# An RWKV-7 recurrence with a SoLU expert layer on one core: only TensorE in a written order, fences as drains, 32-blocks read back from DRAM, decays computed transposed

## The chip, the cores and the metric

The kernel runs on one core of a Trainium2 chip. The metric is device time in microseconds (us) of one execution. The kernel before takes 964.93 us, the median of 3 runs (963.79 to 968.83). All arithmetic is in 32-bit floats. TensorE has two clock levels, 1.2 and 2.4 GHz; the profile's "clock" is the granted share of the higher one.

## The reference

The first half is a recurrence over 768 time steps for 4 batches and 8 heads of dimension 40, on a 40x40 state per head. The second half takes its output, 3072 tokens of 320 numbers, through a layer with an activation, a layer norm and a second matrix.

```python
for t in range(S):                       # S = 768, state [4, 8, 40, 40]
    y[:, :, t] = einsum('bhd,bhde->bhe', r[t], state)
    Sa = einsum('bhde,bhe->bhd', state, a[t])
    state = state * w[t] - einsum('bhd,bhe->bhde', Sa, b[t])
    state = state + einsum('bhd,bhe->bhde', v[t], k[t])

h = x @ w_in                             # [3072, 320] @ [320, 1024]
e = exp(h - max(h))
solu = h * e / (sum(e) + 1e-9)
ln = (solu - mean) / sqrt(var + 1e-6) * g_ln
out = ln @ w_out                         # [3072, 1024] @ [1024, 320]
```

The expert weights come as 64-bit floats; the kernel reads their bits and rebuilds 32-bit floats itself.

## The kernel before

**Chunks.** The 768 steps are cut into 12 chunks of 64, and the 4 batches into 2 pairs, which makes 24 chunk-steps that run one after the other, the two pairs in turn. A pair's two batches lie in the two halves of the 128 partitions. Within a chunk the recurrence becomes small matrix products per batch and head (32 matmuls of one kind at a time, all through the helper `mm`, L212) and a triangular 64x64 solve per batch and head. The solve uses the inverses of the two 32x32 diagonal blocks.

**Names.** `pnt`/`nt` is the triangular matrix of a chunk (`norm`), evicted from PSUM by VectorE. `decay` takes the logarithm of w (`lw`), sums it over time with a matmul (`pcum`) and makes `inv`, its negative exponential, and `ei`, its exponential; four matmuls in `front` turn `ei` into `pex`, which ScalarE copies to `ex`. `kb` (GpSimd) goes to DRAM and comes back rearranged as `kbx`. `px` is the right side of the solve, `x0` its copy (ScalarE), `pu` the solved values, `py` and `pz` the products that build the lower left block of the inverse in `tinvT`. `pyo` holds the chunk's output and the new state; `leave` turns it into `x` and, through four DMAs, `xT`; `tot` and `st` are the new state. `h`, `nmax`, `e`, `bs`, `mv`, `c`, `rs` (GpSimd), `lnT`, `po` and `osb` belong to the expert layer, which runs one and two chunk-steps behind the recurrence.

**Inversion.** The 32x32 blocks of four chunk-steps (4 x 32 of them) make one tile `blk` with a block in each partition. `invert` turns it on VectorE into the inverse `u` with 30 pairs of instructions (`prod`, L358, then `u`, L360), copies its transpose on GpSimd (L363) and writes both to DRAM; `bring` reads the pieces for a step. There are six inversions. Their pieces are laid between the other work by calls `some(k)`. The blocks reach `blk` by six DMAs a step into `blk_dram` (`spread`, L337 and L342) and one load a group (L347).

**Order.** `manual_schedule()` (L83) makes every engine execute its instructions in the order in which the program writes them. The main loop counts i from -9 to 25. Step i begins the matrix work of chunk-step j = i+7 (`norm`), loads its successors, and finishes chunk-step i. For i < 0 only early work is done, and the weights are converted there, five pieces a step (`drawn(5)`). SyncE issues all the DMAs but the weights'.

**Fences.** Before matmuls of another row group add into a PSUM bank, `fence` (L215) puts an empty instruction on GpSimd's queue that takes the bank's tile; TensorE's next matmul then waits for GpSimd to come to it. It stands in `carried` (tiles of `px`) and in the first `read` (tiles of `pyo`), two fences a step. GpSimd works in the program's order too.

Of the kernel before, what the change touches and what calls it, by code (L numbers as in the profile page):

```python
# [45 lines left out]
def kernel(  # L46
# [36 lines left out]
    ctx.enter_context(tc.manual_schedule())  # L83
# [25 lines left out]
    ei_t = zeroed(nc.vector, "ei", [P, H, C], 2, pad)  # L109
    kb_t = zeroed(nc.gpsimd, "kb", [P, 2 * H, C], 2, pad)  # L110
    ex_t = zeroed(nc.vector, "ex", [P, 2, 4, C + 1], AHEAD + 2, lambda x: x[:, :, :, 0:1])
# [21 lines left out]
    def narrow(dst, bits):  # L133
# [4 lines left out]
        def tmp(name):  # L138
            return two.tile([P, 320], I32, tag="n_" + name, name="n_" + name)[0:n, 0:width]

        man, scale, low = tmp("man"), tmp("scale"), tmp("low")
# [89 lines left out]
    def src(ap, i, p):  # L231
        bp, ci = where_(i)
        return ap[2 * bp + p, :, ci * C:(ci + 1) * C, :].rearrange("h t d -> t h d")
# [5 lines left out]
    def load_keys(i, queue=None):  # L239
        if not ok(i):  # L240
            return
        d = st[i]
        for n, ap in (("w", w), ("b", b), ("k", k), ("a", a)):
            x = a_t[i % 3] if n == "a" else two.tile([P, H, D], FP32, tag="raw_" + n, name="raw_" + n)
            d["raw_" + n] = x
            for p in range(2):
                (queue or nc.sync).dma_start(out=x[half(p), :, 0:D], in_=src(ap, i, p))  # L247

    def load_values(i):
        if not ok(i):  # L250
            return
        d = st[i]
        d["v"], d["r"] = v_t[i % 2], r_t[i % 2]
        for n, ap in (("v", v), ("r", r)):
            for p in range(2):
                for h in range(2):
                    nc.sync.dma_start(out=d[n][half(p), 4 * h:4 * h + 4, 0:D], in_=src(ap, i, p)[:, h::2])  # L257


    def decay(i):  # L260
# [3 lines left out]
        lw = two.tile([P, H, D], FP32, tag="lw", name="lw")  # L264
        nc.scalar.activation(out=lw, in_=d["raw_w"], func=AF.Ln)  # L265
        t = bank("pcum")
        nc.tensor.matmul(t[:, 0:DM], lhsT=c_("cum"), rhs=lw, start=True, stop=True)  # L267
        inv = two.tile([P, DM], FP32, tag="inv", name="inv")
        nc.scalar.activation(out=inv, in_=t[:, 0:DM], func=AF.Exp, scale=-1.0)
        d["ei"] = ei_t[i % 2]  # L270
        nc.scalar.activation(out=d["ei"][:, :, 0:D], in_=heads(t[:, 0:DM]), func=AF.Exp)
# [15 lines left out]
    def front(i):  # L287
        if not ok(i):
# [25 lines left out]
    def norm(i):  # L314
# [11 lines left out]
        n, at = i // GRP, (i % GRP) * 32  # L326
        if i % GRP == 0:
            blocks[n] = dram.tile([P, Q, Q], FP32, tag="blk_dram", name="blk_dram", bufs=2)

    def spread(i):  # L330
        if not ok(i):
            return
        nt, n, at = st[i]["nt"], i // GRP, (i % GRP) * 32
        for x in range(2):
            lo = slice(C * x, C * x + Q)
            hi = slice(C * x + Q, C * x + C)
            nc.sync.dma_start(out=blocks[n][at + 8 * x:at + 8 * x + 8].rearrange("h s t -> s h t"),  # L337
                              in_=nt[lo, :, :, 0:Q].rearrange("s h j t -> s (h j) t"))
            base = at + 16 + 4 * x
            gap = 12 if x == 0 else 4  # L340
            for h in range(2):
                nc.sync.dma_start(out=blocks[n][base + gap * h:base + gap * h + 4].rearrange("h s t -> s h t"),  # L342
                                  in_=nt[hi, h, :, Q:])

    def invert(n):
        nb = two.tile([P, Q, Q], FP32, tag="blk", name="blk", bufs=1)
        nc.sync.dma_start(out=nb, in_=blocks[n])  # L347
        u = two.tile([P, Q, Q], FP32, tag="u", name="u", bufs=1)
        flat = u.rearrange("p s t -> p (s t)")
        nc.vector.tensor_scalar(out=flat, in0=nb.rearrange("p s t -> p (s t)"), scalar1=-1.0, scalar2=None,  # L350
                                op0=ALU.mult)
        nc.vector.memset(flat[:, 0:Q * Q:Q + 1], 1.0)
# [9 lines left out]
        ut = nb  # L362
        nc.gpsimd.tensor_copy(out=ut, in_=u.rearrange("p s t -> p t s"))  # L363
        inverse[n] = []
        for name, x in (("u_dram", u), ("ut_dram", ut)):
            x_dram = dram.tile([P, Q, Q], FP32, tag=name, name=name, bufs=2)
            nc.sync.dma_start(out=x_dram, in_=x)
            inverse[n].append(x_dram)
# [3 lines left out]
    def bring(i):  # L372
# [3 lines left out]
        d["ti"], d["ul"], d["uh"] = ti_t[i % 2], ul_t[i % 2], uh_t[i % 2]  # L376
        u, ut = inverse[i // GRP]
        at = (i % GRP) * 32
        for x in range(2):
            lo = slice(C * x, C * x + Q)  # L380
            hi = slice(C * x + Q, C * x + C)
            nc.sync.dma_start(out=d["ul"][lo].rearrange("s h j t -> s (h j) t"),
                              in_=ut[at + 8 * x:at + 8 * x + 8].rearrange("h s t -> s h t"))
            base = at + 16 + 4 * x
            for h in range(2):
                nc.sync.dma_start(out=d["uh"][hi, h], in_=u[base + 8 * h:base + 8 * h + 4].rearrange("h s t -> s h t"))
            nc.sync.dma_start(out=d["ti"][lo, :, :, 0:Q].rearrange("s h j t -> s (h j) t"),
                              in_=u[at + 8 * x:at + 8 * x + 8].rearrange("h s t -> s h t"))
# [8 lines left out]
    def couple(i):  # L397
# [12 lines left out]
    def close(i):  # L410
# [4 lines left out]
        for u in in_turn(lambda p, g, q, h: (p, p ^ h)):  # L415
            p, g, q, h = u
            j = 2 * g + q
            mm(t[h][half(p ^ h), j * Q:j * Q + Q], wy[half(p), h, j], d["uh"][half(p), h, j])
        for h in range(2):
            nc.scalar.copy(out=d["ti"][:, h, :, Q:], in_=t[h][:, 0:4 * Q].rearrange("p (j c) -> p j c", j=4))  # L420


    def attend(i):
# [6 lines left out]
        d["lv"] = two.tile([P, H, W2], FP32, tag="lv", name="lv")  # L430
        nc.gpsimd.tensor_copy(out=d["lv"][:, :, C:], in_=d["v"][:, :, 0:D])
# [21 lines left out]
    def carried(i):  # L453
# [7 lines left out]
        if ci:  # L461
# [6 lines left out]
            fence(d["px"])  # L468
# [14 lines left out]
    def solved(i):  # L483
# [47 lines left out]
    def read(i, own):  # L531
# [212 lines left out]
```

## Time and profile before

| | us |
|---|---|
| median of 3 runs | 964.93 |
| the profiled execution | 965.61 |
| its span | 963.8 |
| TensorE busy | 645.0 |
| VectorE busy | 388.8 |
| ScalarE busy | 248.1 |
| GpSimd busy | 146.9 |
| mean granted clock | 0.787 |

The span goes from the first to the last instruction of the profiled execution. No engine is busy for much more than two thirds of it. The kernel has three stretches: up to the first `h` at 230.7 us, where the early chunk-steps and the weights are prepared; the 24 `h` from 230.7 to 942.8 us, one per chunk-step; and the last 21.0 us. Five of the six inversions lie beside the second stretch. A step is best measured from one start of `h` to the next. TensorE waits seldom long, but the granted clock falls after it has been idle, and then the same matmuls take longer.

### The profile page before, as it was taken

What the parts mean: (1) busy time and instruction counts of PE and PEld (TensorE: products, weight loads), DVE (VectorE), ACT (ScalarE), POOL (GpSimd) and SP (SyncE); (2) the same over time, 40 slices, a digit from 0 to 9 for tenths busy, and PEclk for the clock granted to TensorE, in tenths of its full rate; (3) what the DMA queues carried; (4) which work ended last, traced back from release to release, by engine and by line L of the source; (5) the groups of instructions that cost most, each with busy time, mean ns of one, the idle gap of its engine ahead of it and who ended that gap; (6) DMA issues with size and microseconds to landing.
All of it is one profiled execution on the core that took longest, in us unless ns stands there. A gap on an engine that the chain in (4) does not pass through costs nothing.

```text
span 963.8 us, 27077 instructions
## 1 busy us (share of the span) xinstructions
PE 645.0 (67%) x11449; PEld 479.1 (50%) x11449; DVE 388.8 (40%) x1046; ACT 248.1 (26%) x616; POOL 146.9 (15%) x191
## 2 busy tenths in 40 slices
PE   1422124447797657988287876679893888888886
PEld 1311113435565355666265654556673666666653
DVE  2433464125633095412456330954127442333221
ACT  1322012212333132323123331323220322222211
POOL 4535233000121011011001210110200001000000
PEclk7565555656799869999598998598985877777879
DMA  6545343534344324354143543242431123222000
GB/s 132 141 101 122 90 106 100 108 66 100 85 135 112 77 65 102 63 147 107 40 106 90 138 111 78 65 101 36 130 84 58 27 59 98 56 54 53 20 14 18
DMA packets 245016, 81.86 MB, mean 85 GB/s; under 512 B 227736, under 2 KB 234784, under 8 KB 244896
## 3 DMA queue, kind: packets, MB, share of 16 engines
q1 hardware_dynamic: 242784, 74.64, 33.3%
q10 hardware_dynamic: 2112, 5.49, 1.8%
q8 instruction: 91, 1.49, 0.6%
q14 instruction: 29, 0.24, 0.1%
HBM read 50.19 MB, written 25.95 MB: 79 GB/s over the span
## 4 chain that ended last, share of the span: by engine, by line
PE 26%; issue 22%; DVE 20%; SPq 11%; DMA 9%; POOL 7%; ACT 4%; ACTq 0%; POOLq 0%; DVEq 0%
PE h L599 7%; PE po L649 6%; DVE prod L358 4%; SPq L257 3%; DVE u L360 3%; POOL n_scale L144 2%; PE pyo L212 2%; PE plnT L639 2%; DVE nmax L602 2%; DMA blk<-blk_dram 2%; SPq L247 2%; DMA bits<-in_moe_w_in_dram 2%; DVE e L611 2%; ACT e L605 2%; DVE bs L619 2%
## 5 line engine op out<-in xcount | busy, mean ns | idle before, releaser
L602 DVE TENSOR_REDUCE nmax<-h 128x1 f32<-128x1024 f32 x24 | 29.4, 1223 | 278.1 <-PE h L599 278.1
L599 PE MATMUL h<-w_in,xT 120*128 120x512 f32 (+1 forms) x288 | 136.0, 623 | 0.0
L649 PE MATMUL po<-w,lnT 128*128 128x320 f32 x384 | 114.5, 453 | 0.2 <-ACT lnT L640 0.2
L628 POOL TENSOR_TENSOR rs<-c,mhalf 128x1 f32<-128x1 f32 x24 | 13.7, 571 | 597.0 <-DVE c L627 575.4
L267 PE MATMUL pcum<-lw,cst 128*128 128x320 f32 x48 | 26.6, 647 | 97.4 <-ACT lw L265 97.4
L649 PEld LDWEIGHTS po<-w,lnT 128*128 128x128 f32 x384 | 76.2, 205 | 30.4 <-issue 4.5
L599 PEld LDWEIGHTS h<-w_in,xT 120*128 120x128 f32 (+1 forms) x288 | 55.1, 198 | 62.5 <-issue 59.8
L605 ACT ACTIVATE e<-h,nmax 128x1024 f32<-128x1024 f32 x24 | 26.8, 1116 | 195.6 <-DVE nmax L602 195.6
L212 PE MATMUL pyo<-lv,kbx 64*64 64x104 f32 x768 | 43.6, 295 | 43.5 <-POOLq L217 31.2
L358 DVE TENSOR_TENSOR prod<-blk,u 128x30 f32<-128x30 f32 (+9 forms) x180 | 68.5, 381 | 5.3
L360 DVE TENSOR_TENSOR u<-u,prod 128x30 f32<-128x30 f32 (+9 forms) x180 | 66.0, 367 | 6.2
L350 DVE TENSOR_SCALAR u<-blk 128x1024 f32<-128x1024 f32 x6 | 4.2, 694 | 146.5 <-DMA blk<-blk_dram 146.5
L267 PEld LDWEIGHTS pcum<-lw,cst 128*128 128x128 f32 x48 | 9.6, 250 | 104.5 <-ACT lw L265 104.5
L212 PEld LDWEIGHTS pyo<-lv,kbx 64*64 64x64 f32 x768 | 27.6, 159 | 47.3 <-POOLq L217 33.5
L481 ACT COPY x<-px 128x160 f32<-128x160 f32 x48 | 11.7, 295 | 140.6 <-PE px L212 140.6
L280 PE MATMUL paT<-cst,a 128*104 128x128 f32 x96 | 19.0, 335 | 42.8 <-DVE lu L304 42.8
L212 PE MATMUL px<-lv,psi 64*64 64x40 f32 x768 | 22.2, 275 | 36.9 <-POOLq L217 36.7
L212 PE MATMUL pyo<-lu,kbx 64*64 64x104 f32 x768 | 42.4, 289 | 0.7 <-DVE lu L304 0.5
L639 PE MATMUL plnT<-cst,e 128*128 128x128 f32 x192 | 40.2, 376 | 3.9 <-DVE e L611 3.9
L212 PE MATMUL pnt<-aT,bT 40*64 40x64 f32 x768 | 20.9, 259 | 28.2 <-DVE aT L299 27.7
L212 PEld LDWEIGHTS px<-lv,psi 64*64 64x64 f32 x768 | 19.7, 185 | 39.4 <-issue 34.1
L280 PE MATMUL pkT<-cst,kbx 128*104 128x128 f32 x96 | 22.7, 382 | 23.0 <-DMA kbx<-kb_dram 22.9
(105 smaller groups left out, 1196.3 us busy)
## 6 DMA issues: line engine op xcount, KB each, us to landing
kb_dram<-kb SPq DMA_DIRECT2D x24, 512.0 KB
kbx<-kb_dram SPq DMA_DIRECT2D x24, 512.0 KB
raw_w<-in_w_dram SPq DMA_DIRECT2D x50, 80.0 KB
raw_b<-in_b_dram SPq DMA_DIRECT2D x50, 80.0 KB
raw_k<-in_k_dram SPq DMA_DIRECT2D x50, 80.0 KB
a<-in_a_dram SPq DMA_DIRECT2D x50, 80.0 KB
v<-in_v_dram SPq DMA_DIRECT2D x96, 40.0 KB
r<-in_r_dram SPq DMA_DIRECT2D x96, 40.0 KB
```

Source lines behind the costliest of these rows:

```text
L144: nc.gpsimd.tensor_scalar(out=scale, in0=scale, scalar1=1023 - 127, scalar2=1023 + 128, op0=ALU.max, op1=ALU.min)
L212: nc.tensor.matmul(o, lhsT=lhsT, rhs=rhs, start=start, stop=stop, skip_group_check=True)
L257: nc.sync.dma_start(out=d[n][half(p), 4 * h:4 * h + 4, 0:D], in_=src(ap, i, p)[:, h::2])
L267: nc.tensor.matmul(t[:, 0:DM], lhsT=c_("cum"), rhs=lw, start=True, stop=True)
L280: nc.tensor.transpose(out=t[0:W2, j * P:(j + 1) * P], in_=pair(src_, 2 * j), identity=ident)
L358: nc.vector.tensor_tensor(out=t, in0=nb[:, j:j + 1, j + 1:Q].to_broadcast([P, j, m]), in1=u[:, 0:j, j:j + 1].to_broadcast([P, j, m]), op=A ...
L360: nc.vector.tensor_tensor(out=u[:, 0:j, j + 1:Q], in0=u[:, 0:j, j + 1:Q], in1=t, op=ALU.subtract)
L599: nc.tensor.matmul(h[:, hh], lhsT=d["xT"][0:n, kt, :], rhs=w_in[0:n, kt, hh], start=kt == 0, stop=kt == NK - 1)
L602: nc.vector.tensor_reduce(out=nmax, in_=h, axis=AX.X, op=ALU.max, negate=True)
L605: nc.scalar.activation(out=e, in_=h, func=AF.Exp, bias=nmax, accum_out=d["esum"])
L639: nc.tensor.transpose(out=t[:, j * P:(j + 1) * P], in_=d["e"][:, f * P:(f + 1) * P], identity=ident)
L649: nc.tensor.matmul(o[:, 0:DM], lhsT=d["lnT"][:, f, :], rhs=w2[:, f, :], start=f == 0, stop=f == NF - 1)
```

## The change

Only TensorE keeps the written order. The order of the other engines is set by a scheduler at build time, which is why the rows below and not the diff show it. A fence becomes a drain instruction on TensorE itself. `nt` is written whole to DRAM (one DMA) and its blocks come back into `blk` by four DMAs a step; `blk` has two buffers. v and r are loaded by four DMAs instead of eight and put in order by GpSimd copies. `u` and its transpose lie side by side in one tile, so that `bring` needs four DMAs instead of eight. Of the four xT DMAs two are issued by ScalarE. The output is one DMA. `pex` is computed from `lw` against the summing matrix, so that `ei` and its transposes go. The weights' pieces are drawn in steps -4 to -1, nine a step, the rest in step 0. SyncE issues 26 DMAs in a plain step, before 38.

```diff
-    ctx.enter_context(tc.manual_schedule())
+    ctx.enter_context(tc.manual_schedule(engines={mybir.EngineType.PE}))
...
-    def fence(tiles):
-        for t in tiles:
-            nc.gpsimd.keepalive_nop([nc.gpsimd.lower_ap(t[:, 0:512])])
+    def fence():
+        nc.tensor.drain()
...
+    def in_value_order(i):
...
+        d["v"], d["r"] = v_t[i % 2], r_t[i % 2]
+        d["lv"] = two.tile([P, H, W2], FP32, tag="lv", name="lv")
+        for x, n in ((d["v"][:, :, 0:D], "raw_v"), (d["r"][:, :, 0:D], "raw_r"), (d["lv"][:, :, C:], "raw_v")):
+            nc.gpsimd.tensor_copy(out=x.rearrange("p (h x) d -> p h x d", h=2),
+                                  in_=d[n].rearrange("p (x h) d -> p h x d", h=2))
...
-        nc.scalar.activation(out=d["ei"][:, :, 0:D], in_=heads(t[:, 0:DM]), func=AF.Exp)
+        t = bank("pex")
+        for j in range(4):
+            nc.tensor.matmul(t[0:W2, j * P:(j + 1) * P], lhsT=pair(lw, 2 * j), rhs=c_("cum"), start=True, stop=True)
+        ex = d["ex"] = ex_t[i % (AHEAD + 3)]
+        nc.scalar.activation(out=ex[0:W2, :, :, 1:].rearrange("p b j t -> p j b t"),
+                             in_=t[0:W2].rearrange("p (j b t) -> p j b t", j=4, b=2), func=AF.Exp)
...
+        d["nt_dram"] = dram.tile([P, H, C], FP32, tag="nt_dram", name="nt_dram", bufs=3)
+        nc.sync.dma_start(out=d["nt_dram"], in_=nt.rearrange("p h j c -> p (h j) c"))
...
+        if at == 0:
+            blocks[n] = two.tile([P, Q, Q], FP32, tag="blk", name="blk")
+        for e in range(2):
+            for x in range(2):
+                lo, home = C * x + Q * e, 32 * at + 16 * e + 8 * x
+                nc.sync.dma_start(out=blocks[n][home:home + 8],
+                                  in_=st[i]["nt_dram"][lo:lo + Q, :, Q * e:Q * e + Q].rearrange("s h t -> h s t"))
...
-        nb = two.tile([P, Q, Q], FP32, tag="blk", name="blk", bufs=1)
-        nc.sync.dma_start(out=nb, in_=blocks[n])
+        nb = blocks[n]
+        uu = two.tile([P, Q, 2, Q], FP32, tag="uu", name="uu", bufs=1)
...
+            nc.sync.dma_start(out=d["tu"][lo, :, 0:2 * Q],
+                              in_=uu[at + 8 * x:at + 8 * x + 8].rearrange("h s t -> s h t"))
+            nc.sync.dma_start(out=d["uh"][hi],
+                              in_=uu[at + 16 + 8 * x:at + 24 + 8 * x, :, Q:].rearrange("h s t -> s h t"))
...
-            nc.sync.dma_start(out=xT[2 * D:3 * D, h, :], in_=x[C * h:C * h + D, 3, :])
+            nc.scalar.dma_start(out=xT[2 * D:3 * D, h, :], in_=x[C * h:C * h + D, 3, :])
...
-        if early:
-            drawn(5)
+        if -4 <= i < 0:
+            drawn(9)
...
-        if i == -1:
+        if i == 0:
             drawn(100)
```

**VectorE around an inversion.** Before, in a step that ends a group of four, the inversion begins right behind `nt` (evicted norm), and the step's row maximum of `h`, `nmax`, stands behind its sixth pair. Its beginning:

```order
L583 TENSOR_TENSOR tot<-pyo,st_130 104x4x40 x2
L304 TENSOR_TENSOR nt<-pnt,cst 128x256 x2
L350 TENSOR_SCALAR u<-blk 128x1024
L352 MEMSET u 128x32
L358 TENSOR_TENSOR prod<-blk,u 128x30
```

Eight rows of the same kind follow, and then the sixth pair and `nmax`:

```order
L358 TENSOR_TENSOR prod<-blk,u 128x150
L360 TENSOR_TENSOR u<-u,prod 128x6x25
L602 TENSOR_REDUCE nmax<-h 128x1
L304 TENSOR_TENSOR lu<-pl,cst 128x4x64 x2
L611 TENSOR_TENSOR e<-h,e 128x1024
L304 TENSOR_TENSOR psi<-ps,cst 128x256 x2
```

After, the inversion (on the joint tile `uu`) begins one step later, again right behind `nt`, and `nmax` stands behind 49 of its 62 instructions. Its beginning:

```order
L576 TENSOR_TENSOR tot<-pyo,st_131 104x4x40 x2
L312 TENSOR_TENSOR nt<-pnt,cst 128x256 x2
L353 TENSOR_SCALAR uu<-blk 128x32x32
L354 MEMSET uu 128x32
L360 TENSOR_TENSOR prod<-blk,uu 128x30
```

The place of `nmax`, 46 rows further on:

```order
L362 TENSOR_TENSOR uu<-uu,prod 128x23x8
L360 TENSOR_TENSOR prod<-blk,uu 128x168
L595 TENSOR_REDUCE nmax<-h 128x1
L312 TENSOR_TENSOR lu<-pl,cst 128x4x64 x2
L362 TENSOR_TENSOR uu<-uu,prod 128x24x7
L360 TENSOR_TENSOR prod<-blk,uu 128x150
L604 TENSOR_TENSOR e<-h,e 128x1024
```

So `nmax`, on which `e` and the expert layer of the step rest, has moved from behind the sixth pair to behind the twenty-third; with the step's delay all four quarters of `blk` were loaded a step earlier.

**SyncE between `nt` and `blk`.** Before, in the step that ends a group, the six writes of blocks and the load of the whole stand behind the loads of keys, v and r.

```order
L257 DMA v_124<-in_v_dram 64x4x40 x4
L257 DMA r_120<-in_r_dram 64x4x40 x4
L337 DMA blk_dram<-nt 32x8x32
L342 DMA blk_dram<-nt 32x4x32 x2
L337 DMA blk_dram<-nt 32x8x32
L342 DMA blk_dram<-nt 32x4x32 x2
L347 DMA blk<-blk_dram 128x1024
L395 DMA kbx<-kb_dram 128x1024
```

After, one write of `nt` goes ahead of these loads, and the four reads of blocks behind them; they are there in every step.

```order
L335 DMA nt_dram<-nt 128x512
L232 DMA raw_w<-in_w_dram 64x8x40 x2
L232 DMA raw_b<-in_b_dram 64x8x40 x2
L232 DMA raw_k<-in_k_dram 64x8x40 x2
L232 DMA a_79<-in_a_dram 64x8x40 x2
L232 DMA raw_v<-in_v_dram 64x8x40 x2
L232 DMA raw_r<-in_r_dram 64x8x40 x2
L346 DMA blk<-nt_dram 8x32x32 x4
L390 DMA kbx<-kb_dram 128x1024
```

The loads of v and r have become two of two instead of two of four, and the quarter of `blk` of a step comes in that step.

**ScalarE between `s` and `kT`.** Here `tinvT` (after: `tu`) takes the product `pz`, `x` is the right side copied from `px`, and `xT` the transfer of the step's output. Before:

```order
L529 COPY s<-psT 104x512
L420 COPY tinvT_132<-pz 128x4x32 x2
L481 COPY x_144<-px 128x4x40 x2
L640 COPY lnT<-plnT 128x512 x2
L284 COPY kT<-pkT 104x512
```

After:

```order
L522 COPY s<-psT 104x512
L415 COPY tu_135<-pz 128x4x32 x2
L568 DMA xT<-x 40x128 x2
L474 COPY x_143<-px 128x4x40 x2
L633 COPY lnT<-plnT 128x512 x2
L295 COPY kT<-pkT 104x512
```

Two issues of xT, which wait for VectorE's `x`, now stand ahead of ScalarE's copy of `px` and of `lnT`.

## Rows read from the trace of the kernel before

**Rows 1.** The page, its first line.
```profile
span 963.8 us, 27077 instructions
```

**Rows 2.** Windows cut at starts of h; columns: stretch, its length, busy time, clock, DMA share.
```profile
0.00:230.70 230.70, 80.26 (x1046) 61.27 (x1046) 94.30 (x269) 47.68 (x119) 75.88 (x92) 0.60 0.47 107
365.70:498.40 132.70, 97.98 (x1937) 72.23 (x1929) 58.59 (x154) 38.22 (x98) 15.60 (x21) 0.87 0.41 96
757.20:897.40 140.20, 116.77 (x2185) 89.35 (x2180) 45.76 (x124) 38.01 (x96) 10.40 (x16) 0.81 0.23 57
```

**Rows 3.** Windows: a plain step, a step with the head of an inversion, the tail.
```profile
265.40:291.80 26.40, 22.59 (x489) 16.57 (x483) 8.79 (x23) 10.15 (x28) 5.23 (x6) 1.00 0.46 126
450.60:498.40 47.80, 26.80 (x488) 20.10 (x483) 23.17 (x61) 9.53 (x25) 3.47 (x5) 0.75 0.34 76
942.80:963.80 21.00, 12.49 (x37) 6.74 (x35) 4.28 (x8) 3.33 (x6) 0.55 (x1) 0.90 0.07 16
```

**Rows 4.** Timeline, TensorE, plain step; columns: start, length, instructions, [idle before <-releaser].
```profile
278.20 0.41 PE L212 MATMUL pyo<-lv,kbx 64*64 64x104 f32 x8 [0.47 <-POOLq L217]
...
280.88 0.68 PE L212 MATMUL px<-lv,psi 64*64 64x40 f32 x32 [0.80 <-POOLq L217]
...
291.20 0.66 PE L212 MATMUL py<-ul,nt 64*64 64x32 f32 x30 [1.51 <-DMA ul<-ut_dram]
```

**Rows 5.** Timeline, VectorE, the same plain step.
```profile
270.86 1.23 DVE L602 TENSOR_REDUCE nmax<-h 128x1 f32<-128x1024 f32 x1 [12.95 <-PE h L599]
...
280.47 0.74 DVE L304 TENSOR_TENSOR nt<-pnt,cst 128x256 f32<-128x256 f32 x2
```

**Rows 6.** Waits of the whole span: engine, what waited, releaser, total, times, longest.
```profile
DVE u L350 <- DMA blk<-blk_dram: 146.5, 6, 31.9
...
PE px L212 <- POOLq L217: 36.7, 20, 3.6
...
PE pyo L212 <- POOLq L217: 31.2, 20, 3.3
```

**Rows 7.** Timeline, VectorE, the step with the head of an inversion.
```profile
440.65 0.74 DVE L304 TENSOR_TENSOR nt<-pnt,cst 128x256 f32<-128x256 f32 x2
468.95 0.69 DVE L350 TENSOR_SCALAR u<-blk 128x1024 f32<-128x1024 f32 x1 [27.55 <-DMA blk<-blk_dram]
...
473.05 1.22 DVE L602 TENSOR_REDUCE nmax<-h 128x1 f32<-128x1024 f32 x1
...
480.57 1.04 DVE L358 TENSOR_TENSOR prod<-blk,u 128x184 f32<-128x184 f32 x1
```

**Rows 8.** Timeline, SyncE's queue, the same step.
```profile
465.76 0.34 SPq L347 DMA_DIRECT2D blk<-blk_dram  x1
```

**Rows 9.** Timeline, TensorE, the same step.
```profile
474.65 1.10 PE L280 MATMUL paT<-cst,a 128*104 128x128 f32 x4 [16.04 <-DVE lu L304]
```

**Rows 10.** Groups of instructions, VectorE; count, busy time, mean ns of one.
```profile
L358 DVE TENSOR_TENSOR prod<-blk,u 128x30 f32<-128x30 f32 (+9 forms) x180 | 68.5, 381 | 5.3
L360 DVE TENSOR_TENSOR u<-u,prod 128x30 f32<-128x30 f32 (+9 forms) x180 | 66.0, 367 | 6.2
```

**Rows 11.** Timeline, TensorE, a step from 757 us on.
```profile
827.92 0.62 PE L212 MATMUL pyo<-lv,kbx 64*64 64x104 f32 x8 [3.30 <-POOLq L217]
```

**Rows 12.** Groups of instructions, TensorE: the matmuls behind the second fence.
```profile
L212 PE MATMUL pyo<-lv,kbx 64*64 64x104 f32 x768 | 43.6, 295 | 43.5 <-POOLq L217 31.2 <-DVE lu L304 11.4 <-ACT ei L271 0.9
```

**Rows 13.** Groups of instructions, GpSimd: the copy of v.
```profile
L431 POOL COPY lv<-v 128x320 f32<-128x320 f32 x24 | 11.1, 461 | 2.2 <-DMA v<-in_v_dram 2.2
```

**Rows 14.** Timeline, VectorE, first inversion, before the main loop.
```profile
103.67 0.69 DVE L350 TENSOR_SCALAR u<-blk 128x1024 f32<-128x1024 f32 x1 [7.93 <-DMA blk<-blk_dram]
```

**Rows 15.** Timeline, TensorE, from the first inverse to the first h.
```profile
167.74 0.39 PE L212 MATMUL py<-ul,nt 64*64 64x32 f32 x2 [1.63 <-DMA ul<-ut_dram]
...
189.13 1.07 PE L280 MATMUL pkT<-cst,kbx 128*104 128x128 f32 x4 [11.28 <-DMA kbx<-kb_dram]
...
214.73 0.44 PE L212 MATMUL pyo<-lv,kbx 64*64 64x104 f32 x2 [11.42 <-DVE lu L304]
```

More of the change, by code (lines that the diff above doesn't have):

```diff
@@ L229, in where_, with load, load_keys @@
         return i % NPAIR, i // NPAIR
-    def src(ap, i, p):
+    def load(x, ap, i):
         bp, ci = where_(i)
-        return ap[2 * bp + p, :, ci * C:(ci + 1) * C, :].rearrange("h t d -> t h d")
+        for p in range(2):
+            nc.sync.dma_start(out=x[half(p), :, 0:D],
+                              in_=ap[2 * bp + p, :, ci * C:(ci + 1) * C, :].rearrange("h t d -> t h d"))
     def ok(i):
         return 0 <= i < N
-    def load_keys(i, queue=None):
+    def load_keys(i):
         if not ok(i):
@@ L245, in load_keys @@
             d["raw_" + n] = x
-            for p in range(2):
-                (queue or nc.sync).dma_start(out=x[half(p), :, 0:D], in_=src(ap, i, p))
+            load(x, ap, i)
     def load_values(i):
@@ L252, in load_values @@
         d = st[i]
+        for n, ap in (("v", v), ("r", r)):
+            d["raw_" + n] = two.tile([P, H, D], FP32, tag="raw_" + n, name="raw_" + n)
+            load(d["raw_" + n], ap, i)
+    def in_value_order(i):
+        if not ok(i):
+            return
+        d = st[i]
         d["v"], d["r"] = v_t[i % 2], r_t[i % 2]
[L254 to L257, printed above, removed]
+        d["lv"] = two.tile([P, H, W2], FP32, tag="lv", name="lv")
+        for x, n in ((d["v"][:, :, 0:D], "raw_v"), (d["r"][:, :, 0:D], "raw_r"), (d["lv"][:, :, C:], "raw_v")):
+            nc.gpsimd.tensor_copy(out=x.rearrange("p (h x) d -> p h x d", h=2),
+                                  in_=d[n].rearrange("p (x h) d -> p h x d", h=2))
     def decay(i):
@@ L361, in invert @@
             yield
-        ut = nb
         nc.gpsimd.tensor_copy(out=ut, in_=u.rearrange("p s t -> p t s"))
[L364 to L368, printed above, removed]
+        inverse[n] = dram.tile([P, Q, 2 * Q], FP32, tag="uu_dram", name="uu_dram", bufs=2)
+        nc.sync.dma_start(out=inverse[n], in_=uu.rearrange("p s two t -> p s (two t)"))
         yield
@@ L649, in output @@
             nc.tensor.matmul(o[:, 0:DM], lhsT=d["lnT"][:, f, :], rhs=w2[:, f, :], start=f == 0, stop=f == NF - 1)
-        osb = two.tile([P, DM], FP32, tag="osb", name="osb")
+        osb = two.tile([P, DM], FP32, tag="osb", name="osb", bufs=1)
         nc.scalar.activation(out=osb, in_=o[:, 0:DM], func=AF.Copy, scale=d["rs"])
-        for p in range(2):
-            row = (2 * bp + p) * S + ci * C
-            nc.sync.dma_start(out=out[row:row + C, :], in_=osb[half(p)])
+        nc.sync.dma_start(out=out.rearrange("(b s) n -> b s n", b=B)[2 * bp:2 * bp + 2, ci * C:ci * C + C], in_=osb)
     inv, wts = [None], weights()
@@ L674 @@
             load_keys(0)
-            load_keys(1)
         carried(i)
```

86 lines of the change are left out of this document (29 added, 57 removed).

## The prediction

> **What bounds the kernel now.** I read the span first [rows 1], then windows cut at starts of `h` [rows 2], one step without and one with the head of an inversion [rows 3], and last the timelines of the engines in these. Three things are to be seen. The first `h` comes at 230.7 us, and TensorE is busy for 80 of these at a clock of 0.60. A cycle of four steps takes 132.7 us, of which a step with the head of an inversion takes 47.8 and a plain one 26.4: 3 x 26.4 + 47.8 = 127, and the rest is in the step behind the head. And from 757 us on, where no early work is left, five steps take 140.2 us, 28.0 each, longer than the plain step with all its early work, at a clock of 0.81 against 1.00.
>
> In the plain step TensorE is busy for 22.59 of 26.40 us, so it is the bound, and 3.81 us are gaps. Three of them are 0.47 and 0.80 us behind the fences and 1.51 us at `py`, which waits for a piece of the inverse that SyncE sent late [rows 4]. Over the span the fences hold TensorE for 36.7 + 31.2 us, up to 3.6 us at a time [rows 6]: GpSimd reaches the empty instruction only when it has done what stands ahead of it. In the late steps one such gap is 3.30 us [rows 11]. In the step with the inversion's head VectorE has `nt` at 441.39, then waits 27.55 us for `blk`, runs six pairs and starts `nmax` at 473.05 [rows 7], whereas TensorE stands 16.04 us at `paT`, behind `lu`, which is queued behind `nmax` [rows 9]. The load of `blk` is issued at 465.76, 24.4 us behind `nt`, because SyncE's queue holds the loads of the inputs first [rows 8].
>
> **The change, part by part.** All sums are for the profiled execution, 965.61 us, which is 1.8 over its span and 0.7 over the median.
>
> *Drains.* A plain step has two; the one in `carried` is absent in the first chunks, so there are 22 + 24 = 46. No drain is in the trace. From below the cost is 0 (GpSimd's fences could only be met at once). The nearest row for the inside of one is a `pyo` matmul, 0.295 us [rows 12], which must end before the next starts, while consecutive ones overlap; with the next weight load uncovered I take 0.45 us. The upper end is the present gap, 3.30 us. So 46 x 0.45 = 20.7 us, and 0 to 152 as bounds.
>
> The Trainium skill ("TensorE: Matmul & The Clock Gate", section "Single matmul latency") gives an isolated matmul of N columns (398 + N) / 2.4 ns at the high clock. By that an uncovered one of 104 columns would be 0.21 us and the 46 drains 9.6 us, 11 us less than by the row; no row here shows an isolated one.
>
> *A plain step with early work.* 26.40 - 1.51 (SyncE issues 26 DMAs a step instead of 38, so the pieces of the inverse leave earlier) - 0.47 - 0.80 (the two old fences) + 2 x 0.45 = 24.5 us. The new order of ScalarE puts two issues of xT ahead of `x0` and `lnT`; I cost them at nothing, since TensorE works on `pnt` and `pyo` meanwhile; without that cover they are rival B. One transpose group and one ScalarE exponential go, four `pex` matmuls take the place of four transposes: no change. Of the steps from the first `h` on, 14 are of this kind (343 us), and the two in which the early work ends take 23.0 each (46).
>
> *Late steps.* Five at 28.0 before. Minus 3.30 and about 1.5 at the other fence (36.7 / 20 is 1.8), plus 0.9, that is 24.1 at a clock of 0.81. Without the gap the clock should stay at the plain step's 1.00. 23.35 us of busy time a step at 0.81 [rows 2] would shrink by some 3.6 us, to 20.5. I take the middle, 22.2: five are 111. The last two, 45.4 us before (897.4 to 942.8), I put at 38 by the same ratio and a little more, since the recurrence is done there. Steps together: 343 + 46 + 111 + 38 = 538 us.
>
> *Inversions.* Each starts one step later, with `blk` long there, so the 27.55 us are gone. But 49 of its 62 instructions now run before `nmax`. A pair takes 0.381 + 0.367 us [rows 10]; 30 pairs are 22.4 us, with 0.04 us between instructions 24.8, or 0.41 each, so 48 of them and the first (0.69 [rows 7]) take 20.5 us. In the plain step `nt` ends 281.21 - 270.86 = 10.4 us after `nmax` starts [rows 5], so the inversion ends its 49 at 30.9 us, whereas the next `h` ends 24.5 us after the last: `nmax` is 6.4 us late, and TensorE idle about that long. Behind such a gap the clock falls: the step with the 16.04 us gap shows 26.80 us of busy time against 22.59 [rows 3], 4.2 more. Pieces ahead of `x` cost another 1.5. Together 12.1.
>
> GpSimd gets two copies more, v and r. The row beside its `kb` shows what GpSimd's work does to the inversion: a `prod` of 128x184 takes 1.04 us [rows 7] where the mean is 0.381, so it is stretched by about 0.66. Each copy takes 0.461 us [rows 13]; with two more and `lv` beside the inversion, 0.9 us. Per inversion 13, and five lie beside the main loop: 5 x 13 = 65 us.
>
> The Trainium skill ("GPSIMD Engine Reference", section "1. Specifications") has the cause: GpSimd's SBUF interfaces are shared with VectorE, with contention for VectorE instructions with two SBUF inputs. The trace agrees, with 1.04 us beside 0.381. By that rule VectorE's evictions from PSUM go free, and the new copies cost nothing in steps without an inversion; charged to every VectorE instruction beside them, as one might from the row alone, they would be 24 x 2 x 0.46 = 22 us more.
>
> *Before the first `h`.* The first inversion starts at 103.67 after 7.93 us for `blk` [rows 14], and TensorE reaches `py` at 167.74 [rows 15], 64 us later, because its pieces lie among the weights' work. In the new order it is nearly one run: from about 95 us, 25 us of it, then a transposed copy, a write and a read (about 12), so `py` at about 132. Then it is held by the weights: the last of them are drawn in step 0 and I expect them at 155. From `py` to the first `h` it is 63 us now, with gaps of 11.28 and 11.42 us [rows 15]; after the weights some 33 of it remain. So 188, a saving of 43. Bounds: 160 (the weights hide) to 230 (nothing is won).
>
> *Rest.* The tail, 21.0 [rows 3], is as it was. For waits that a free order brings and that I can't name I add 0.5 us to 22 steps, 11.
>
> Sum: 188 + 538 + 65 + 11 + 21 = 823 of span, with 1.8 and less 0.7 that is 824; I forecast 822 us.
>
> **The rivals.**
>
> *A. The inversion hides no better than now.* If 49 instructions in one stretch cost as much as now, that is 25 us a cycle over 4 plain steps (132.7 - 4 x 26.9), five times 12 more than I have: about 882. For it: `nmax` is the head of the whole expert layer, and it now stands behind four times as many pieces. Against: the wait of 27.55 us was for the transfer.
>
> *B. ScalarE's queue.* The xT issues wait for VectorE's `x`; `px`'s copy and `lnT` stand behind them. If each step loses 2.5 us at this place, 22 x 2.5 = 55: 877. For it: ScalarE is in order. Against: the copy of `px` waits for the same stretch of work anyway.
>
> *C. No shorter start.* The weights' work is moved behind, not shortened; if the first `h` stays at 230.7: 865.
>
> *D. Slower, by drains.* Each drain empties TensorE twice a step, and after an empty spell the clock may stay low, as in the late steps (0.81 with one gap of 3.30 a step). If a drain costs 3.30 us and the step's clock 3.6 us over two drains, 5.1 each, 46 x (5.1 - 0.45) = 214 more: 1036. It decides from 3.5 us a drain on, where 46 drains use up the 142 + 21 us that all else wins. Against: the fence waits now contain GpSimd's work, which a drain doesn't wait for.
>
> *E. The inversions hide wholly* and the start is at 170: 822 - 55 - 18 = 749.
>
> *F. It does not do what it says:* VectorE and SyncE may wait elsewhere for the same transfers: 965, no change.
>
> **How the numbers follow.** Forecast 822 (own range 765 to 860): 0.50. A 0.13, B 0.10, C 0.10, E 0.07, D 0.07, F 0.03. The range from 755 to 890 takes in A, B and C whole and leaves out D, F and E in part. No change is within 0.5%, about what a measurement here can tell: 0.03. Slower is D, 0.07; the others are faster, 0.90.
>
> **What would show it.** The first `h` near 188. Plain steps near 24.5 us with TensorE gaps under a microsecond at the two drains, no wait for GpSimd's queue at `px` and `pyo`. Late steps near 22 us at a clock near 1.00. No wait of VectorE for `blk`; one gap of about 6 us in TensorE an inversion, released by `lu`. It is wrong where the drains' gaps are over a microsecond, where ScalarE's `x0` is late behind xT, where the clock stays near 0.8 in steps without an inversion, or where the start is not shorter.

## The result, and the profile after

The changed kernel takes 824.7 us (4 runs, 821.3 to 830.8), the kernel before 966.1 on the same chip: a ratio of 0.854 (95%: 0.849 to 0.860). The forecast was 822. The times of kernels are medians of all their runs; the ratios leave out the three runs that lay over 1.5% above the fastest of the same kernel (one of e3, two of e8), so they can differ a little from the quotient of the medians.

The page of the changed kernel, its first line and TensorE's; TensorE's busy time, 644.9 us, is what it was in the table of the kernel before (645.0), in a span of 819.5 us instead of 963.8 [rows 1]:

```profile
span 819.5 us, 26810 instructions
...
PE 644.9 (79%) x11545; PEld 480.8 (59%) x11545; DVE 379.0 (46%) x1048; ACT 239.8 (29%) x592; POOL 168.4 (21%) x237
```

Windows of the changed kernel, cut at starts of `h`: the start; two cycles of four steps; a plain step; a step with the head of an inversion; three late steps; the tail. The columns are those of [rows 2]:

```profile
0.00:178.70 178.70, 84.38 (x1089) 67.59 (x1089) 91.33 (x257) 46.97 (x111) 78.68 (x96) 0.64 0.61 143
290.90:400.10 109.20, 97.74 (x1946) 73.78 (x1945) 54.51 (x154) 36.86 (x93) 19.12 (x29) 0.97 0.52 120
400.10:509.70 109.60, 98.21 (x1946) 73.60 (x1944) 55.82 (x155) 36.99 (x94) 19.00 (x29) 0.97 0.53 120
459.20:484.60 25.40, 23.94 (x491) 18.00 (x488) 8.66 (x23) 9.07 (x23) 4.21 (x7) 1.00 0.56 122
400.10:431.90 31.80, 26.52 (x488) 19.67 (x486) 20.87 (x59) 9.15 (x24) 6.26 (x8) 0.89 0.43 94
650.20:733.20 83.00, 68.62 (x1313) 50.52 (x1309) 22.19 (x60) 22.45 (x59) 6.74 (x13) 0.88 0.17 44
795.40:819.50 24.10, 13.06 (x37) 7.38 (x35) 4.17 (x8) 3.43 (x6) 0.55 (x1) 0.79 0.04 14
```

The first `h` comes at 178.7 us (230.7 before), a cycle takes 109 us (132.7), the plain step 25.4 (26.4), the step with an inversion's head 31.8 (47.8). But the three late steps, which have the least to do, take 83.0, 27.7 each, at a clock of 0.88.

In the plain step the two old fence gaps [rows 4] are gone; no gap of TensorE in it is over 0.52 us. One is 0.23 us at `pz`, in front of which a drain stands (the second drain, ahead of `pnt`, shows 0.12 us); the longest is a wait for `kbx`:

```profile
471.11 1.07 PE L211 MATMUL pz<-uh,wy 64*64 64x32 f32 x28 [0.23 <-DVE c L618]
...
476.84 0.62 PE L291 MATMUL pkT<-cst,kbx 128*104 128x128 f32 x4 [0.52 <-DMA kbx<-kb_dram]
```

VectorE and TensorE around an inversion, changed kernel, answering to [rows 7, 9]: `uu` starts right behind `nt` without the 27.55 us, `nmax` follows 19.1 us later, and TensorE's gap is 3.56 us where it was 16.04.

```profile
390.21 0.76 DVE L312 TENSOR_TENSOR nt<-pnt,cst 128x256 f32<-128x256 f32 x2
390.88 0.68 DVE L353 TENSOR_SCALAR uu<-blk 128x1024 f32<-128x1024 f32 x1
...
410.02 1.21 DVE L595 TENSOR_REDUCE nmax<-h 128x1 f32<-128x1024 f32 x1
```

TensorE, behind that `nmax`:

```profile
411.62 1.44 PE L274 MATMUL pcum<-lw,cst 128*128 128x320 f32 x2 [3.56 <-DVE lu L312]
```

And TensorE's largest wait in all was not among my terms of the steps. Two of its 17 pieces, 13.54 and 2.71 us, lie ahead of the first `h`, and 26.5 us behind it (the columns are total, times, longest):

```profile
PE pkT L291 <- DMA kbx<-kb_dram: 42.7, 17, 13.5
```

### The profile page after: what moved, and what is told of

It reads as the page before. It is cut to its first block, busy times and chain, and to the rows that moved or that the text cites. A ratio compares the mean times of both kernels' runs of the same rounds, so it can differ in the third digit from the quotient of the medians.

```text
span 819.5 us, 26810 instructions
## 1 busy us (share of the span) xinstructions
PE 644.9 (79%) x11545; PEld 480.8 (59%) x11545; DVE 379.0 (46%) x1048; ACT 239.8 (29%) x592; POOL 168.4 (21%) x237
## 4 chain that ended last, share of the span: by engine, by line
PE 46%; DVE 23%; DMA 15%; issue 5%; POOL 5%; ACT 3%; SPq 2%; ACTq 0%; DVEq 0%; POOLq 0%
PE h L592 14%; PE po L642 10%; DMA kbx<-kb_dram 7%; DVE prod L360 5%; DVE uu L362 5%; PE pz L211 3%; PE pyo L211 3%; DVE e L604 3%; DVE nmax L595 3%; PE py L211 3%; DVE bs L612 2%; DMA uu_dram<-uu 2%; PE pu L211 2%; POOL n_s L143 2%; ACT e L598 2%
## 5 line engine op out<-in xcount | busy, mean ns | idle before, releaser
L360 DVE TENSOR_TENSOR prod<-blk,uu 128x30 f32<-128x30 f32 (+9 forms) x180 | 62.9, 350 | 6.0
L362 DVE TENSOR_TENSOR uu<-uu,prod 128x30 f32<-128x30 f32 (+9 forms) x180 | 61.5, 342 | 5.7
L285 POOL TENSOR_TENSOR kb<-raw_b,inv 128x320 f32<-128x320 f32 x24 | 20.9, 869 | 151.4 <-ACT inv L276 131.1
L291 PE MATMUL pbT<-cst,kb 128*104 128x128 f32 x96 | 18.4, 323 | 39.5 <-POOL kb L285 39.5
L263 POOL COPY v<-raw_v 128x320 f32<-128x320 f32 x24 | 10.9, 456 | 179.8 <-DMA raw_v<-in_v_dram 179.7
L291 PEld LDWEIGHTS pkT<-cst,kbx 128*104 128x104 f32 x96 | 12.2, 154 | 50.0 <-issue 46.9
L644 ACT ACTIVATE osb<-po,rs 128x320 f32<-128x320 f32 x24 | 12.7, 527 | 94.5 <-PE po L642 94.5
L211 PE MATMUL py<-tu,nt 64*64 64x32 f32 x768 | 30.6, 227 | 8.2 <-DMA tu<-uu_dram 6.0
L279 PEld LDWEIGHTS pex<-cst,lw 128*104 128x104 f32 x192 | 32.8, 223 | 7.0 <-issue 4.1
L474 ACT COPY x<-px 128x160 f32<-128x160 f32 x48 | 11.7, 295 | 83.7 <-PE plnT L632 25.4
L291 PEld LDWEIGHTS pbT<-cst,kb 128*104 128x104 f32 x96 | 11.4, 149 | 41.8 <-POOL kb L285 40.5
```

What stands on the lines that cost most here:

```text
L211: nc.tensor.matmul(o, lhsT=lhsT, rhs=rhs, start=start, stop=stop, skip_group_check=True)
L279: nc.tensor.matmul(t[0:W2, j * P:(j + 1) * P], lhsT=pair(lw, 2 * j), rhs=c_("cum"), start=True, stop=True)
L285: nc.gpsimd.tensor_tensor(out=kb[:, j * H:j * H + H, 0:D], in0=d["raw_" + n], in1=heads(inv), op=ALU.mult)
L291: nc.tensor.transpose(out=t[0:W2, j * P:(j + 1) * P], in_=pair(src_, 2 * j), identity=ident)
L360: nc.vector.tensor_tensor(out=t, in0=nb[:, j:j + 1, j + 1:Q].to_broadcast([P, j, m]), in1=u[:, 0:j, j:j + 1].to_broadcast([P, j, m]), op=A ...
L362: nc.vector.tensor_tensor(out=u[:, 0:j, j + 1:Q], in0=u[:, 0:j, j + 1:Q], in1=t, op=ALU.subtract)
```

## The experiments

The two kernels differ in the order of four engines and in eight edits (the drains, the blocks through `nt`, v and r, the joint inverse, two xT issues on ScalarE, the single output DMA, `pex`, the weights' place), so I first took these apart. Not every edit was run by itself, nor was ScalarE's order. "Written" is the program's order, "free" the scheduler's; TensorE is as written in all.

| kernel | free engines | edits | us | ratio to before, 95% |
|---|---|---|---|---|
| e4 | none | drains alone | 919.5 | 0.951 (0.948 to 0.954) |
| e1 | none | all | 929.7 | 0.963 (0.958 to 0.969) |
| e5 | VectorE | none | 874.1 | 0.905 (0.902 to 0.907) |
| e6 | GpSimd | none | 926.6 | 0.957 (0.953 to 0.961) |
| e7 | SyncE | none | 934.9 | 0.967 (0.964 to 0.971) |
| e2 | all but TensorE | none | 829.8 | 0.860 (0.856 to 0.863) |
| changed | all but TensorE | all | 824.7 | 0.854 (0.849 to 0.860) |
| e3 | all but TensorE | all but drains | 817.8 | 0.841 (0.837 to 0.845) |
| e12 | all but TensorE | none, new `kbx` | 808.8 | 0.837 (0.833 to 0.841) |
| e9 | all but TensorE | all, third `kbx` buffer, earlier place | 775.0 | 0.802 (0.797 to 0.806) |
| e8 | all but TensorE | all, new `kbx` | 770.3 | 0.794 (0.791 to 0.796) |
| e10 | as e8 | 48 drains more | 791.3 | 0.816 (0.810 to 0.822) |
| e11 | as e8 | 28 of 30 pairs left out | 754.0 | 0.778 (0.773 to 0.782) |

**e1: the edits without the order.**

```diff
-    ctx.enter_context(tc.manual_schedule(engines={mybir.EngineType.PE}))
+    ctx.enter_context(tc.manual_schedule())
```

> The changed kernel with the order of every engine as written; all other edits stay. My theory: the free order is worth a good part, because nmax then stands again behind a step's wait for blk. The four reads of blk stand in SyncE's queue behind 12 loads (about 9 us of issue) instead of 16 loads and 6 writes, so VectorE waits about 14 us instead of 27.5 in each of five steps, and the narrowing of the weights before the first h is serial again (first h near 210). Drains stay. I expect 885 us, 860 to 915. Rival 1, the edits alone make the gain and the order none: 825. Rival 2, the order is the whole gain: 960.

929.7 us: between my value and rival 2. Its first `h` comes at 235.6 us, as late as before, so in the written order the later drawing of the weights brings the start nothing. VectorE waits for `blk` again, 18 us each time, more than the 14 I had from the shorter queue:

```profile
DVE uu L353 <- DMA blk<-nt_dram: 91.2, 5, 21.1
```

**e2: the order without the edits.** The same line, put into the kernel before.

> The kernel before with the one line of the order changed: only TensorE as written. My theory: the inversions move behind the landed blk and the start is interleaved, but the fences still hold TensorE for GpSimd's queue and the pieces of the inverse still need eight DMAs. I expect 885 us, 850 to 920, with the waits for GpSimd's queue at px and pyo still over 40 us together. Rival 1 (the order is nothing): 965. Rival 2 (the order is all): 830.

829.8 us, rival 2. My theory fell: the order alone gives 138 us where the whole change gives 141, and the two ratios can't be told apart (0.856 to 0.863 and 0.849 to 0.860). The waits of e2 show how. VectorE's wait for `blk` and the fence waits [rows 6] shrink to about a fifth and a third, with neither drains nor another way for the blocks; a wait for `kbx` has grown in their place, from 22.9 us before:

```profile
PE pkT L280 <- DMA kbx<-kb_dram: 84.7, 15, 19.7
...
DVE u L350 <- DMA blk<-blk_dram: 27.9, 4, 13.9
...
PE pyo L212 <- POOLq L217: 12.8, 14, 1.7
...
PE px L212 <- POOLq L217: 9.5, 7, 1.7
```

**e3: the changed kernel with fences on GpSimd's queue.**

```diff
-    def fence():
-        nc.tensor.drain()
+    def fence(tiles):
+        for t in tiles:
+            nc.gpsimd.keepalive_nop([nc.gpsimd.lower_ap(t[:, 0:512])])
```

> The changed kernel with the fences on GpSimd's queue as before. My theory: the fences cost TensorE 68 us of idle time before, and 46 drains cost about 10; with the lower clock behind the longer gaps the drains are worth about 50 us, so I expect 875 us, 850 to 900. Rival: in a free order GpSimd comes to the empty instruction at once, and the drain is worth nothing: 825.

817.8 us (811 to 829), not slower than with drains: the rival. These runs overlap with those of the changed kernel (821 to 831), so the two can't be ranked closely. In a free order the same empty instructions cost TensorE 13 us, where they cost 68:

```profile
PE px L211 <- POOLq L216: 9.2, 9, 1.4
...
PE pyo L211 <- POOLq L216: 4.2, 11, 0.5
```

**e4: the kernel before with drains.**

```diff
-        for t in tiles:
-            nc.gpsimd.keepalive_nop([nc.gpsimd.lower_ap(t[:, 0:512])])
+        nc.tensor.drain()
```

> The kernel before with drains for fences, every order as written, nothing else changed. My theory: the idle time at the fences (68 us over the span) goes but for some 10 us, part of it returns as other waits, and in the late steps the clock stays high: I expect 905 us, 880 to 935. Rival: the fences only stood where another wait was due anyway (lv from VectorE, st from GpSimd): 955 to 965.

919.5 us, 48 less, within my range. So the drains are worth 48 us in a written order and nothing in a free one: they remove a wait that was GpSimd's order, and the scheduler removes the same. It is also 10 us less than e1, so in the written order the other seven edits together cost 10 us. Three late steps of e4 take 65.2 us, 21.7 each, at a clock of 1.00, where they took 27.4 before at 0.81:

```profile
795.50:860.70 65.20, 60.31 (x1313) 43.60 (x1308) 22.54 (x60) 21.51 (x55) 5.03 (x9) 1.00 0.30 66
```

**e5, e6, e7: one engine free at a time**, in the kernel before. The set names the other four, which stay as written.

```diff
-    ctx.enter_context(tc.manual_schedule())
+    ctx.enter_context(tc.manual_schedule(engines={...}))
```

> The kernel before with VectorE's order alone left to the scheduler; TensorE, ScalarE, GpSimd and SyncE as written, fences on GpSimd's queue. The runs so far say that the free order is the whole gain (830 us with it alone). My theory now: most of it is VectorE's: the inversion begins a step later, behind a blk that has landed. I expect the waits of u for blk to fall from 146 us to under 40, an excess per inversion of some 10 us instead of 25, and a start some 25 us shorter: 870 us, 850 to 895; the fence waits stay near 68. Rival: the order of GpSimd carries the gain, and this gives over 930.

874.1 us, as expected. Its waits: `blk` is down to 14.6 us, the fences stay near where they were [rows 6].

```profile
PE pyo L212 <- POOLq L217: 36.3, 22, 3.5
...
PE px L212 <- POOLq L217: 30.0, 22, 4.6
...
DVE u L350 <- DMA blk<-blk_dram: 14.6, 3, 9.5
```

> The kernel before with GpSimd's order alone left to the scheduler, so that the empty instructions of the fences can stand elsewhere in its queue. My theory: the fence waits fall from 68 us to about 20, and the time to what drains gave there (919 us): 925 us, 905 to 945; the waits for blk stay near 146. Rival 1: the fences stay where they are because their tiles bind them, 965. Rival 2: GpSimd's order carries the whole gain, under 870.

926.6 us, as expected. The fence waits fall to a quarter:

```profile
PE px L212 <- POOLq L217: 9.1, 6, 1.6
...
PE pyo L212 <- POOLq L217: 7.6, 12, 1.3
```

TensorE and GpSimd in one of its late steps: `pyo` runs at 802.93 without a gap, 3.3 us before GpSimd comes to `rs`, whereas in the kernel before TensorE stood there for 3.30 us [rows 11]; so the empty instruction must stand ahead of `rs` now. The fence at `px` still waits, 1.61 us, until `rs` runs:

```profile
802.93 0.39 PE L212 MATMUL pyo<-lv,kbx 64*64 64x104 f32 x8
...
806.61 0.76 PE L212 MATMUL px<-lv,psi 64*64 64x40 f32 x32 [1.61 <-POOLq L217]
```

GpSimd, the same step:

```profile
806.27 0.55 POOL L628 TENSOR_TENSOR rs<-c,mhalf 128x1 f32<-128x1 f32 x1 [21.12 <-DVE c L627]
806.77 0.45 POOL L431 COPY lv<-v 128x320 f32<-128x320 f32 x1
```

> The kernel before with SyncE's order alone left to the scheduler. In it the load of blk still stands behind the loads of the inputs and behind the output and kb_dram. My theory: it brings little, 955 us, 935 to 970, because VectorE's inversion still stands in front of nmax and waits for blk about as long. Rival: a shorter queue brings blk early and this gives under 900.

934.9 us, 32 less: more than I expected, not enough for the rival. VectorE's wait for `blk` falls from 146.5 to 106.5 us. The three gains, 93, 40 and 32, would be 165 us together; all four orders at once, ScalarE's among them, give 138. So VectorE's order is worth most. That the sum is not reached can have two reasons which no run separates: partly they remove the same idle time, and all at once they bring the wait for `kbx` in e2 (84.7 us; 26 to 33 in these three).

**e8: `kbx`.** The three late steps led here. One of them in the changed kernel, timelines; GpSimd:

```profile
690.68 0.55 POOL L621 TENSOR_TENSOR rs<-c,mhalf 128x1 f32<-128x1 f32 x1 [18.25 <-PE px L211]
691.18 0.45 POOL L263 COPY lv<-raw_v 128x320 f32<-128x320 f32 x1
```

SyncE's queue:

```profile
691.66 0.67 SPq L232 DMA_DIRECT2D raw_v<-in_v_dram  x1
692.42 0.81 SPq L390 DMA_DIRECT2D kbx<-kb_dram  x1
```

TensorE:

```profile
697.46 1.06 PE L291 MATMUL pkT<-cst,kbx 128*104 128x128 f32 x4 [5.85 <-DMA kbx<-kb_dram]
```

GpSimd's `lv` copy waits behind `rs` and ends at 691.6. Only then is the buffer of `raw_v` free, and SyncE issues that load, and behind it, at 692.42, `kbx`. TensorE waits 5.85 us for it and then runs `pkT` in 1.06 us instead of 0.62, at the lower clock.

But the queue is only half of this wait. `kbx` has two buffers, and the load of one chunk-step goes into the buffer that `pyo` of two chunk-steps earlier still reads; here the last of these matmuls ends at 689.36. So the queue costs 3.1 of the 5.85 us; the rest would have been there without it, since it is 5.0 us from the issue to `pkT`. In the plain step the queue costs nothing: SyncE issues the load as soon as `pyo` has ended, at 473.07. TensorE's last `pyo`, then SyncE:

```profile
472.82 0.25 PE L211 MATMUL pyo<-lu,kbx 64*64 64x104 f32 x1
```

```profile
473.10 0.34 SPq L390 DMA_DIRECT2D kbx<-kb_dram  x1
```

Over the span SyncE itself stands at this load, and all behind it in the queue with it:

```profile
SPq L390 <- PE pyo L211: 137.8, 17, 12.9
```

e8 gives `kbx` a third buffer (`nt` and `xT` have one less each for it), an earlier place in the program, and ScalarE's queue.

```diff
-        d["kb"] = two.tile([P, 2 * H, C], FP32, tag="kbx", name="kbx")
-        nc.sync.dma_start(out=d["kb"], in_=d["kb_dram"])
+        d["kb"] = two.tile([P, 2 * H, C], FP32, tag="kbx", name="kbx", bufs=3)
+        nc.scalar.dma_start(out=d["kb"], in_=d["kb_dram"])
...
+        fetch(i + 2)
         load_keys(j + 3)
...
-        fetch(i + 2)
```

> The changed kernel with a third buffer for kbx (paid for by one buffer less of xT and of nt) and its load issued by ScalarE, ahead of SyncE's queue of loads. In the changed kernel TensorE waits 42.7 us at pkT for kbx, 5.2 and 5.9 us in two late steps where the load stands behind a load of v that waits for its buffer. My theory: these waits go, and the clock in the late steps comes back to near 1.00: 795 us, 780 to 810. Rival: ScalarE's queue holds kbx as late as SyncE's did, or a later wait takes the place: 820 to 830.

770.3 us (6 runs, 765 to 779), 54 less than the changed kernel and below my range. The wait is gone; late steps take 22.4 us (four of them, 89.6) and plain ones 24.1 to 25.0, and the clock is back:

```profile
616.50:706.10 89.60, 84.44 (x1748) 60.59 (x1744) 29.58 (x80) 28.49 (x77) 8.57 (x16) 1.00 0.19 50
```

ScalarE issues `kbx` in such a step here, with none of SyncE's loads ahead of it:

```profile
672.58 0.33 ACTq L390 DMA_DIRECT2D kbx<-kb_dram  x1
```

**e9: buffer or queue?** e8 with one line back.

```diff
-        nc.scalar.dma_start(out=d["kb"], in_=d["kb_dram"])
+        nc.sync.dma_start(out=d["kb"], in_=d["kb_dram"])
```

> The kernel of e8 with one line back: kbx has its third buffer, but SyncE issues its load again. In the late steps the load stands behind a load of v in SyncE's queue, in the steps with early work ahead of the loads of keys. My theory: both halves count. The buffer takes away the waits of the steps with early work, the late ones stay: 800 us, 785 to 815, with three waits of pkT for kbx over 2 us behind 615 us. Rival 1, the queue is all: 820. Rival 2, the buffer is all: 770.

775.0 us, close to rival 2: the buffer, with the earlier place in the program that both runs have, does nearly all, and ScalarE's queue at most some 5 us. No run separates buffer and place, but without a third buffer the load can't start before `pyo` has ended, whatever its place. In the late steps of e9 SyncE issues `kbx` 19 to 27 us ahead of its `pkT`, where it was 4 to 5 in the changed kernel, so a place in the queue that is some us late no longer shows. The three late waits that I expected are not there.

**e10: the price of a drain.** A third and fourth drain in each step of e8, ahead of `pu` and of `h`.

```diff
+        if 0 <= i < N:
+            fence()
         solved(i)
...
+        if 0 <= i < N:
+            fence()
         hidden(i - 1)
```

> The kernel of e8 with two drains more in each of the 24 steps, between py and h and between po and pu, where TensorE is otherwise busy without a gap: 48 more. It prices a drain by itself. My theory now, from the gaps of about 0.23 us behind the drains of the changed kernel: 48 x 0.23 = 11 us more than e8, 781. Rival 1, my forecast's 0.45 us: 792. Rival 2, a drain lowers the clock behind it (my slower case, 5.1 us each): over 900.

791.3 us, 21 more or 0.44 each, if all of it is theirs; the runs (781.7 to 793.1) spread by half of that. Ahead of `h` the gap itself is 0.22 us, below, and a late step in which nothing else is late grows from 22.4 to 22.7 us, 0.15 for each of its two drains; the rest is in steps with early work. The mean clock is 0.884 against 0.894, so rival 2 is out. My 0.23 is right for the gap and too small for the whole.

```profile
679.71 5.40 PE L592 MATMUL h<-w_in,xT 120*128 120x512 f32 x12 [0.22 <-issue]
```

**e11: what the inversions still cost.** From e8.

```diff
-        for j in range(1, Q - 1):
+        for j in range(1, 3):
```

> The kernel of e8 with 2 of the 30 pairs of each inversion; the other 28 are left out of the computation. It prices what the six inversions still cost. My theory: from the spread of its steps (29 to 30 us with an inversion's head, some 24.1 without) five inversions cost 31 us beside the main loop and the first some 15 before it: 725 us, 710 to 740. Rival 1, my forecast's 13 us each: 690. Rival 2, they are hidden: 765.

754.0 us, 16 less than e8: none of the three. The stretch from the first `h` to the last shrinks from 566.7 to 557.5 us, though VectorE works 88 us less in it. Some e11 steps are longer than the same steps of e8 (29.0 us for 24.1, and 26.4 for 24.1; I have not followed up why), so 16 is what leaving the pairs out gains, not what each step with a pair loses. The windows of the main loop, of e8:

```profile
178.50:745.20 566.70, 529.15 (x10422) 394.03 (x10422) 281.32 (x783) 186.25 (x475) 91.45 (x140) 0.97 0.44 102
```

And of e11; VectorE's is the third busy time:

```profile
171.20:728.70 557.50, 523.98 (x10423) 388.74 (x10422) 192.95 (x521) 186.60 (x475) 86.56 (x139) 0.98 0.44 102
```

**e12: the kernel before, free order, new `kbx`.** The line of e2 and the diff of e8 in the kernel before.

> The kernel before with only TensorE as written (as e2) and kbx as in e8: third buffer, load issued by ScalarE. Fences on GpSimd's queue, eight DMAs for the inverses, six for the blocks, decays as before. My theory: the other edits are worth little once the order is free (830 against 825 us without the new kbx), so this comes near e8: 785 us, 765 to 805. Rival: they are worth what they relieve on SyncE, and show once kbx is out of the way: over 815.

808.8 us, between the two. With `kbx` out of the way the other edits are worth 808.8 - 770.3 = 38 us; with `kbx` in the way some 5 (829.8 to 824.7), no more than the runs differ. What they relieve shows in e12's waits:

```profile
DVE u L350 <- DMA blk<-blk_dram: 54.2, 5, 19.9
...
PE py L212 <- DMA ul<-ut_dram: 31.9, 8, 15.7
```

## Why the prediction was right, and where it was not

**The sum came out, its terms only in part.** Each term, forecast and measured:

| term | forecast | measured |
|---|---|---|
| first `h` | 188 | 178.7 |
| plain step | 24.5 + 0.5 | 25.1 to 25.4 |
| excess per inversion | 13 | about 9 |
| four late steps, no inversion (without the 0.5) | 88.8 | 105.9 |
| tail | 21.0 | 24.1 |

Put together as the sum was: the start came 9 us under the forecast, the first 16 steps with four inversions 12 under (436.9 us for 449), the last seven with one inversion 15 over (179.7 for 165), the tail 3 over. That these cancel to 3 us is luck.

**The start.** Shorter by 52 us rather than 43. `py` came at 126.8 us (132 forecast) and the last of the weights at 154.5 (155); the error is in what follows, 24 us to the first `h` instead of 33. A reason failed too: I had the weights' new place as part of it; e1, which has that place and a first `h` at 235.6, and e2, which has it not and 182.3, show that the order does it. VectorE's order alone gives 203.3 (e5), SyncE's 219.6 (e7), GpSimd's 229.8 (e6).

**Plain steps.** Right. The gaps behind the old fences and at `py` went, the drains' are 0.23 and 0.12 us, and 0.5 us is the wait for `kbx`, within what I had added for waits I could not name.

**Inversions.** The mechanism was right: `blk` has landed, `nmax` is late behind 49 pieces, TensorE idles and the clock dips (0.89 over that step). The sizes were too large: the stretch from `uu` to `nmax` took 19.1 us, not 20.5, and TensorE's gap was 3.56 us, not 6.4. The step costs 31.8 - 25.4 = 6.4 us, the next 27.3 - 25.4 = 1.9; a cycle of 109.2 or 109.6 us less four plain steps of 25.1 is about 9. Rival A is out. My 0.66 us for GpSimd beside the inversion came from a mean over ten shapes: the trace of the kernel before has the same 128x184 `prod` at 1.04 us beside `kb` (in three inversions) and at 0.35 us by itself (in the other three), so the size was about right; whether the new copies cost it no run shows.

**Late steps: the failed step.** I took the fence's gap out and nothing in. Of five late steps the first holds the last inversion (34.6 us); the others took 28.2, 29.7, 25.0 and 23.0 us, not 22.2, three of them at a clock of 0.88 where I had 1.00. What I had counted is right by itself: e4, with the drains and the old order, has three of these steps at 21.7 us and a clock of 1.00. What I put at nothing was `kbx`: its load waits for the last reader of its buffer, and in the new order also stands behind a load that waits for another. With that wait removed in e8 they take 22.4: the 22.2 was right for a step that nothing is late in. I had read SyncE's new order where it mattered for `blk`, and not in the late steps, where its loads run ahead until a full buffer stops the queue. (In the working, the clock from 0.81 to 1.00 would by its rows give back 23.35 x 0.19 = 4.4 us, not 3.6; that moves the middle to 21.8 only.)

**The tail.** I took it as unchanged. It is 23.8 to 25.0 us in all seven kernels with the single output DMA and 20.7 to 21.7 in all seven with two: behind ScalarE's last `osb` the span lasts 6.4 us in the changed kernel, 3.8 in the kernel before.

**The drains.** 0.45 us was the upper side of what e10 shows (0.15 to 0.44), and rival D, slower by drains, is out. The gap in e10 is 0.22 us. The figure that I had from the Trainium skill ("TensorE: Matmul & The Clock Gate", section "Single matmul latency"; an estimate of 0.21 us for 104 columns) is near that gap, but the page gives it for a bf16 matmul on the full array, and these are 32-bit ones on a quarter of it. But I credited the drains with the fences' gaps, and e3 shows that in this order they are worth nothing. The forecast could not tell them apart, because either alone removes the wait.

**Rivals B and C** did not come: the issues of xT cost ScalarE 1.5 us a step, but e8, with a third issue there, is faster; and the start was shorter. E (749 us) and F (no change) did not come either.

## What to carry to other kernels

Where the engines' queues are written by hand, ask of every long wait whether the thing waited for was late or only queued behind something else: here the queues' order alone, VectorE's above all, gave 138 of the 141 us, and the edits to the work itself added no more to it than the runs differ. An edit that gives nothing may be hidden by a larger wait: they gave 38 once that was gone. After a free order read each queue in the stretch with the least work too, and ask when each load's buffer comes free: a load that waits for a buffer holds all behind it, and a third buffer for the one that is on the path, with an earlier place in the program, was worth 50 us (e9).

## What the hardware showed unexpectedly

Taking `kbx`'s wait away was worth more than the wait. The 16.2 us of it ahead of the first `h` gave nothing: in e8 a wait of 22.1 us for `v` stands in their place, and the first `h` comes at 178.5 us, not 178.7. But the stretch from the first `h` to the last is 50 us shorter in e8, 566.7 for 616.6, though only 26.5 us of waits lay in it. Of the rest, 18 us are TensorE's busy time, 547.4 against 529.2, at a mean clock of 0.93 against 0.97: behind a gap the matmuls run at the lower clock, as `pkT` shows with 1.06 us behind the 5.85 us gap and 0.62 behind one of 0.52. The remaining 5 us or so are other gaps. The stretch in the changed kernel, to be held against that of e8 above:

```profile
178.73:795.37 616.64, 547.38 (x10422) 405.83 (x10422) 283.46 (x784) 189.38 (x475) 89.21 (x140) 0.93 0.40 95
```
